# A new order of issue, a fifth buffer for turned probabilities, and the bucket table in the halves' pool, in an attention and two-MoE kernel

## The chip, the cores and the metric

One core of one Trainium2 chip runs the whole kernel in one launch. The metric is device time in microseconds (us). The kernel before was timed three times: 784.86 median (784.70, 784.86, 785.94).

## What is computed

Three stages in a chain, all in float32:

```python
# 1. attention over hash buckets: q, k, v (2, 8, 768, 64), proj (64, 6)
q_bucket = sum(((q @ proj) > 0) * 2**arange(6));  k_bucket likewise
scores = where(q_bucket == k_bucket, q @ k.T / 8, -1e9)
x = softmax(scores) @ v                      # -> (1536, 512)
# 2. first MoE layer, 512 -> 1536 -> 512
xn = x / sqrt(mean(x*x) + 1e-6) * rms_g
g = xn @ w_gate
x = (g * sigmoid(g) * (xn @ w_val)) @ w_out
# 3. second MoE layer, 512 -> 2048 -> 512
h = x @ w_in
out = where(h > 0, h, exp(min(h, 0)) - 1) @ w2_out
```

## The kernel before

Each float32 operand of a matmul is split into a rounded high part (`hi`) and the rest (`lo`), and a product takes three matmuls: hi with hi, hi with lo, lo with hi. The high part is mostly cast by ScalarE (ACT), the rest mostly subtracted by VectorE (DVE), some of both by GpSimd (POOL).

**Attention** goes over 8 pairs of heads, each with 6 units of 2 x 128 query rows. A unit is: TensorE (PE) makes the scores (`score`, L612) in PSUM; DVE takes the negative row maximum `nm` (L619); ACT the exponentials `p` (L629); PE turns `p` in three groups of four 128x128 transposes (`turn`, L657); ACT casts a turned group into a `pt` tile (L665) and DVE subtracts the rest into the same tile (L669), or for one group of some units POOL does both (L678, L681); PE multiplies by the values (`weigh`, L704). The bucket mask is made by a table of bucket counts, `wsel`: PE multiplies bits by it (`prep_count`, L539) and the result is cast into extra rows of the query and key operands (ACT L550, DVE L552). The operands' other rows come from casts and subtractions (for the first pair ACT L479 and L482, DVE L486 and L489; later queries POOL L451 and L462).

**The MoE layers** take tokens in four blocks of 384 columns and hidden features in tiles of 128. A few hidden tiles are computed plainly; the others in a Strassen-like scheme (`pair`, 9 in the first layer, 6 in the second), whose products add up in `ps_wA`, `ps_wC`, `ps_wE` (L1511). For a plain tile of the second layer, `hidden` runs: PE `ps_h` (L1060), ACT exponential and relu (L1088, L1097), DVE `hf` (L1101, "d3"), ACT cast of `h` (L1107), DVE rest of `h` (L1111). The first layer's output is reduced in `reduce1`: PE `ps_y` (L1151), DVE adds it into `ya` (L1163); with the last part added, ACT casts `y2` (L1168) and DVE subtracts the rest (L1172). The second layer's output is reduced in `reduce_cols`: PE `ps_o` (L1211), ACT copies it into `oa` (L1220) or DVE adds (L1224). `spread_t` makes differences of `ya` blocks (L1251, the first four of them on POOL) and splits them (ACT L1258, POOL L1262) for the second layer's pairs. Between the layers, plain groups 1 and 2 of the second layer (two hidden tiles each) run while the last reductions of the first layer end: the **hand-over**, some 500 to 560 us into the span. Raw weights are rounded word by word: ACT L957 ("top"), POOL L960, DVE L966, L973 and L980 (called **c3, c4, c5** here), then ACT L1005 and POOL L1009 make `whi` and `wlo`.

**The order.** `Plan.add` collects 3568 tasks with what they read and write. They are emitted in the order of a table of numbers, `ORDER` (L36):

```python
def run(self):
    assert sorted(ORDER) == list(range(len(self.tasks)))
    for i in ORDER:
        self.tasks[i][2]()
```

Each engine runs its own instructions in that order, and the tile pools add the waits for buffers. The pools that matter here:

```python
SLOTS, H3S, PTS = 22, 15, 4
...
big = ctx.enter_context(tc.tile_pool(name="big", bufs=SLOTS))
ptp = ctx.enter_context(tc.tile_pool(name="ptp", bufs=PTS))
hlf = ctx.enter_context(tc.tile_pool(name="hlf", bufs=H3S))
...
st[T_] = ptp.tile([128, 2, 512], F32R, tag="pt", name="pt")
```

`ptp` holds the `pt` tiles in attention and the `h` tiles of plain hidden tiles afterwards. `hlf` holds "halves": raw loads of queries, keys and values, POOL's `pf`, the attention output `ot`, the raw table and others. In PSUM there are two double banks (`ps_s`; for the MoE layers `ps_y` or `ps_o`) and four single banks (`ps_p`, `ps_v`, `ps_c`, `ps_h`, `ps_w...`).

Of the kernel before, what the change touches and what calls it, by code (L numbers as in the profile page):

```python
# [20 lines left out]
SLOTS, H3S, PTS = 22, 15, 4  # L21
# [254 lines left out]
def kernel(  # L276
# [41 lines left out]
    def half(shape, dtype, name):  # L318
        return hlf.tile(shape, dtype, tag="h3", name=name)
# [40 lines left out]
    def mm(n):  # L360
        return (n + 31) / 2400.0

    def dma(fn, nbytes, r=(), w=(), prio=None):
        return plan.add("SP", max(0.5, nbytes / 315e3), fn, r, w, prio, 2.3)

    st = {}

    RAW = ("qk", "kk", "qq")

# [1457 lines left out]
```

## Time and profile before

| what | value |
|---|---|
| median of 3 runs | 784.86 us |
| the profiled execution | 783.64 us, of it the span 781.9 us |
| PE busy, share of the span | 770.5 us, 99% |
| DVE, ACT, POOL busy | 663.8 (85%), 527.5 (67%), 470.8 (60%) us |
| clock granted to TensorE, mean | 1.000 |

The span runs from the first instruction to the last. Busy time is the union of an engine's instructions; matmuls are pipelined and their ends are modelled, so a row's duration can reach over the next row's start, and the starts tell more exactly when PE went on. The profiled execution is 1.22 us below the median.

### The profile page before, as it was taken

What the parts mean: (1) busy time and instruction counts of PE and PEld (TensorE: products, weight loads), DVE (VectorE), ACT (ScalarE), POOL (GpSimd) and SP (SyncE); (2) the same over time, 40 slices, a digit from 0 to 9 for tenths busy, and PEclk for the clock granted to TensorE, in tenths of its full rate; (3) what the DMA queues carried; (4) which work ended last, traced back from release to release, by engine and by line L of the source; (5) the groups of instructions that cost most, each with busy time, mean ns of one, the idle gap of its engine ahead of it and who ended that gap; (6) DMA issues with size and microseconds to landing.
All of it is one profiled execution on the core that took longest, in us unless ns stands there. A gap on an engine that the chain in (4) does not pass through costs nothing.

```text
span 781.9 us, 12995 instructions
## 1 busy us (share of the span) xinstructions
PE 770.5 (99%) x4618; PEld 726.0 (93%) x4618; DVE 663.8 (85%) x1067; ACT 527.5 (67%) x1094; POOL 470.8 (60%) x480
## 2 busy tenths in 40 slices
PE   8999999999999999999999999999999999999998
PEld 7999999989999999999999999988899889988996
DVE  7898999999995956887877887898998888898786
ACT  7999999999985536654544455567776666666652
POOL 6998889899796185554455566336364353533520
PEclk9999999999999999999999999999999999999999
DMA  4646753361010002212221122410041121131104
GB/s 169 217 141 218 255 158 106 102 183 42 6 50 1 1 1 81 82 55 74 62 80 55 55 82 81 130 60 27 1 135 54 37 72 55 54 106 56 54 1 161
DMA packets 33648, 65.73 MB, mean 84 GB/s; under 512 B 3504, under 2 KB 13104, under 8 KB 33584
## 3 DMA queue, kind: packets, MB, share of 16 engines
q1 hardware_dynamic: 33584, 64.91, 25.9%
q8 instruction: 36, 0.59, 0.3%
q14 instruction: 28, 0.23, 0.1%
HBM read 56.25 MB, written 3.15 MB: 76 GB/s over the span
## 4 chain that ended last, share of the span: by engine, by line
PE 89%; DVE 7%; ACT 2%; issue 1%; DMA 1%; SPq 0%; DVEq 0%; ACTq 0%
PE ps_o L1211 17%; PE ps_wA L1511 16%; PE ps_y L1151 12%; PE ps_h L1060 9%; PE ps_wC L1511 8%; PE ps_s L612 7%; PE ps_v L704 7%; PE ps_p L657 7%; PE ps_wE L1511 4%; DVE nm L619 1%; DVE y L1172 1%; DVE pt L669 1%; PE ps_x L762 1%; PE ps_b L520 1%; ACT p L629 1%
## 5 line engine op out<-in xcount | busy, mean ns | idle before, releaser
L1211 PE MATMUL ps_o<-whi,h 128*128 128x512 f32 (+1 forms) x388 | 119.4, 389 | 1.3 <-ACT oa L1220 1.3
L1449 POOL TENSOR_TENSOR W<-wf,W 128x256 fp32r<-128x256 f32 x105 | 85.9, 830 | 53.4 <-ACT W L1445 49.5
L1151 PE MATMUL ps_y<-h,whi 128*128 128x384 f32 x528 | 107.6, 336 | 1.1 <-DVE ya L1163 0.9
L1511 PE MATMUL ps_wA<-T,W 128*128 128x384 f32 x540 | 108.0, 335 | 0.0
L1511 PEld LDWEIGHTS ps_wA<-T,W 128*128 128x128 f32 x540 | 95.3, 188 | 2.4 <-ACT wt L1529 0.3
L1151 PEld LDWEIGHTS ps_y<-h,whi 128*128 128x128 f32 x528 | 92.5, 188 | 3.1 <-DVE ya L1163 2.5
L619 DVE TENSOR_REDUCE nm<-ps_s 128x1 f32<-128x768 f32 x96 | 90.9, 948 | 4.2 <-PE ps_s L612 3.5
L704 PE MATMUL ps_v<-pt,vv 128*128 128x256 f32 x576 | 92.8, 292 | 0.0
L629 ACT ACTIVATE p<-ps_s,nm 128x768 f32<-128x768 f32 x96 | 87.3, 910 | 2.7 <-DVE nm L619 1.6
L612 PE MATMUL ps_s<-tk,tq 128*128 128x384 f32 x384 | 87.8, 351 | 1.2 <-ACT p L629 1.2
L669 DVE TENSOR_TENSOR pt<-ps_p,pt 128x512 fp32r<-128x512 f32 x120 | 80.6, 682 | 6.1 <-ACT pt L665 4.9
L657 PE MATMUL ps_p<-ident,p 128*128 128x128 f32 x576 | 84.2, 274 | 1.0 <-DVE pt L669 0.7
L1211 PEld LDWEIGHTS ps_o<-whi,h 128*128 128x128 f32 x388 | 71.8, 188 | 13.7 <-ACT oa L1220 1.6
L704 PEld LDWEIGHTS ps_v<-pt,vv 128*128 128x128 f32 x576 | 78.2, 189 | 1.5 <-issue 0.6
L1368 POOL TENSOR_SCALAR wf<-wf 128x512 f32<-128x512 f32 x51 | 36.5, 719 | 71.5 <-ACT wf L1365 62.0
L1211 PE MATMUL ps_o<-wlo,h 128*128 128x512 f32 (+1 forms) x194 | 76.0, 392 | 0.0
L665 ACT CAST pt<-ps_p 128x512 fp32r<-128x512 f32 x120 | 69.5, 591 | 7.7 <-PE ps_p L657 4.7
L657 PEld LDWEIGHTS ps_p<-ident,p 128*128 128x128 f32 x576 | 66.9, 140 | 7.7 <-DVE pt L669 2.6
L1435 POOL TENSOR_TENSOR wf<-wf 128x256 f32<-128x256 f32 x60 | 50.1, 835 | 39.5 <-DVE wf L1384 34.3
L1224 DVE TENSOR_TENSOR oa<-ps_o,oa 128x512 f32<-128x512 f32 (+1 forms) x85 | 57.4, 679 | 17.6 <-PE ps_o L1211 17.2
L612 PEld LDWEIGHTS ps_s<-tk,tq 128*128 128x128 f32 x384 | 63.5, 189 | 4.5 <-ACT p L629 3.1
L1163 DVE TENSOR_TENSOR ya<-ps_y,ya 128x384 f32<-128x384 f32 x80 | 43.2, 551 | 15.5 <-PE ps_y L1151 15.0
(159 smaller groups left out, 1795.0 us busy)
## 6 DMA issues: line engine op xcount, KB each, us to landing
wraw<-in_moe_w_out_dram SPq DMA_DIRECT2D x25, 512.0 KB, 3.4
wraw<-in_moe_w_in_dram SPq DMA_DIRECT2D x16, 512.0 KB, 3.9
qk<-in_heads_dram SPq DMA_DIRECT2D x16, 384.0 KB, 5.2
kk<-in_heads_dram SPq DMA_DIRECT2D x14, 384.0 KB, 5.5
qq<-in_heads_dram SPq DMA_DIRECT2D x14, 384.0 KB, 5.7
wraw<-in_moe_w_gate_dram SPq DMA_DIRECT2D x18, 256.0 KB, 2.8
wraw<-in_moe_w_val_dram SPq DMA_DIRECT2D x18, 256.0 KB, 3.1
tq<-tq SPq DMA_DIRECT2D x21, 192.0 KB, 3.0
```

The lines of the kernel that those rows point to most:

```text
L612: nc.tensor.matmul(st[B_][:, hf, 0:HS], lhsT=tq[:, x, c * 128:(c + 1) * 128], rhs=tk[:, x, hf * HS:(hf + 1) * HS], start=(x == 0), stop=(x ...
L619: nc.vector.tensor_reduce(out=st["nm", u, cc], in_=st[B_][:, :, 0:HS], axis=AX.XY, op=ALU.max, negate=True,)
L629: nc.scalar.activation(out=halves(st["p", u][:, cc]), in_=st.pop(B_)[:, :, 0:HS], func=AF.Exp, bias=st["nm", u, cc], scale=1.0, accum_out= ...
L657: nc.tensor.transpose(out=st[B_][:, o:o + 128], in_=p[:, cc, (2 * n + kt) * 128:(2 * n + kt + 1) * 128], identity=ident,)
L665: nc.scalar.copy(out=st[T_][:, 0], in_=st[B_])
L669: nc.vector.tensor_tensor(out=pt[:, 1], in0=st.pop(B_), in1=f(pt[:, 0]), op=ALU.subtract)
L704: nc.tensor.matmul(st[B_][:, 0:256], lhsT=st["vv", j][:, a, 2 * n + kt, :], rhs=pt[:, x, kt * 256:(kt + 1) * 256], start=(n == seq[0] and ...
L1060: nc.tensor.matmul(ps[:, o:o + ln], lhsT=(w[wp][kk // 2][:, kk % 2] if reg2(g) else w[wp][:, kk])[:, ft * 128:(ft + 1) * 128], rhs=t[xp][: ...
L1151: nc.tensor.matmul(s["ps"][:, 0:bw], lhsT=wo[wp][:, ft if g == 0 else 0, m * 128:(m + 1) * 128], rhs=h[:, xp, 0:bw], start=(ft == 0 and i ...
L1211: nc.tensor.matmul(s["ps"], lhsT=h[:, xp, t * 128:(t + 1) * 128], rhs=(wo[wp][ft][:, 0] if reg2(g) else wo[wp][:, ft])[:, ds], start=(ft = ...
L1449: nc.gpsimd.tensor_tensor(out=t[:, 1], in0=blk(*src), in1=f(t[:, 0]), op=ALU.subtract)
L1511: nc.tensor.matmul(s[bk], lhsT=w[:, wp, k], rhs=x[:, xp, cs], start=start and k == 0 and i == 0, stop=k == 1 and i == 2, skip_group_check= ...
```

## The change

Four things change:

- `PTS` goes from 4 to 5.
- `wsel` (128 x 512 words, 2 KB a partition) is no longer a constant tile but takes one of the 15 halves, from the start until the last bucket count of the last pair of heads.
- The second plain group of the second layer takes the token blocks in the order 1, 3, 0, 2, as the first does, instead of 0, 2, 1, 3.
- `ORDER` is wholly new. It holds the same 3568 tasks, and each engine issues as many instructions of each kind as before.

```diff
-SLOTS, H3S, PTS = 22, 15, 4
+SLOTS, H3S, PTS = 22, 15, 5
...
-    wsel = const.tile([128, 2, 2, 128], F32R, name="wsel")
...
+    wsel = half([128, 2, 2, 128], F32R, "wsel")
...
-        plan.add("PE", mm(HS) + 0.02, pe, [("bits", j), "wsel"], [B_], prio)
+        plan.add("PE", mm(HS) + 0.02, pe, [("bits", j), ("h3", "wsel")], [B_], prio)
...
-    plan.add("DVE", 2.9, setup_bits, [], ["floor", "wzero"], -29)
+    plan.add("DVE", 2.9, setup_bits, [], ["floor", ("h3", "wsel")], -29)
...
-    plan.add("ACT", 0.75, spread_table, [("h3", "wtmp"), "wzero"], ["wsel"], -28)
+    plan.add("ACT", 0.75, spread_table, [("h3", "wtmp")], [("h3", "wsel")], -28)
...
-        for n, blk in enumerate((1, 3, 0, 2) if g == 1 else (0, 2, 1, 3)):
+        for n, blk in enumerate((1, 3, 0, 2) if NPW[0] % 2 else (0, 2, 1, 3)):
...
 ORDER = [
-    1, 8, 3, 0, 6, 45, 9, 7, 5, 10, 11, 12, 13, 14, 42, 43, 44, 24, 25, 2, 54, 15, 16, 71, 47, 17, 28, 29, 46, 48,
+    0, 3, 2, 1, 8, 9, 10, 11, 12, 13, 14, 15, 6, 45, 42, 44, 43, 7, 54, 5, 28, 29, 47, 49, 24, 55, 71, 16, 17, 18,
...
```

`NPW[0]` is 9 here. What the table moves at three places of the hand-over follows. A number behind a name tells tiles of one name apart; numbers of before and after are not the same.

**ScalarE, group 1 of the second layer.** `ps_o` are the first output parts of that layer, `oa` their copies, `sg`, `h` and `T` belong to hidden tiles and to the spread. Before:

```order
L1107 CAST h_6720<-hf_6680 128x384
L1088 ACTIVATE sg_6723<-ps_h_6634 128x384
L1097 ACTIVATE sg_6723<-sg_6723,ones_85 128x384
L1258 CAST T_6727<-ya_3917 128x768
L1107 CAST h_6732<-hf_6730 128x384
L1088 ACTIVATE sg_6749<-ps_h_6647 128x384
L1097 ACTIVATE sg_6749<-sg_6749,ones_85 128x384
L1088 ACTIVATE sg_6753<-ps_h_6660 128x384
L1258 CAST T_6755<-ya_3788 128x768
L1097 ACTIVATE sg_6753<-sg_6753,ones_85 128x384
L1220 COPY oa_6759<-ps_o_6683 128x512
L1220 COPY oa_6759<-ps_o_6690 128x512
```

After:

```order
L1088 ACTIVATE sg_6734<-ps_h_6656 128x384
L1107 CAST h_6736<-hf_6683 128x384
L1097 ACTIVATE sg_6734<-sg_6734,ones_84 128x384
L1107 CAST h_6742<-hf_6697 128x384
L957 ACTIVATE wf_6745<-wraw_6627 128x512
L1220 COPY oa_6749<-ps_o_6674 128x512
L1220 COPY oa_6749<-ps_o_6685 128x512
L1088 ACTIVATE sg_6753<-ps_h_6643 128x384
L957 ACTIVATE wf_6756<-wraw_6549 128x512
L1097 ACTIVATE sg_6753<-sg_6753,ones_84 128x384
L1258 CAST T_6763<-ya_3863 128x768
```

The two copies of `oa` stood behind the exponentials and relus of both hidden tiles that PE computes just before the first `ps_o`, and behind two spreads of `T`; now they stand behind those of one of these tiles and a conversion (L957), and the other tile and the `T` come after them.

**VectorE, the end of the first layer's reductions.** The last part of a weight is converted (L966, L973, L980) between adds of `ps_y`. Before:

```order
L1163 TENSOR_TENSOR ya_3917<-ps_y_6405,ya_3917 128x384
L966 TENSOR_SCALAR wf_6312<-wf_6312 128x512
L1579 TENSOR_TENSOR hf_6315<-hf_6315,wt_6380 128x384
L973 SCALAR_TENSOR_TENSOR wf_6312<-wraw_6277,wf_6312 128x512
L1163 TENSOR_TENSOR ya_3788<-ps_y_6414,ya_3788 128x384
L980 SCALAR_TENSOR_TENSOR wf_6312<-wraw_6277,wf_6312 128x512
L1163 TENSOR_TENSOR ya_3788<-ps_y_6429,ya_3788 128x384
L1579 TENSOR_TENSOR hf_6443<-ps_wA_6323,wt_6354 128x384
L1163 TENSOR_TENSOR ya_3857<-ps_y_6452,ya_3857 128x384
L1172 TENSOR_TENSOR y2_6424<-ya_3917,y2_6424 128x384
```

After:

```order
L966 TENSOR_SCALAR wf_6374<-wf_6374 128x512
L1579 TENSOR_TENSOR hf_6359<-hf_6359,wt_6381 128x384
L973 SCALAR_TENSOR_TENSOR wf_6374<-wraw_6331,wf_6374 128x512
L1163 TENSOR_TENSOR ya_3863<-ps_y_6391,ya_3863 128x384
L1532 TENSOR_TENSOR wt_6344<-ps_wE_6413,wt_6344 128x384
L1163 TENSOR_TENSOR ya_3759<-ps_y_6422,ya_3759 128x384
L980 SCALAR_TENSOR_TENSOR wf_6374<-wraw_6331,wf_6374 128x512
L1172 TENSOR_TENSOR y2_6430<-ya_3759,y2_6430 128x384
L1579 TENSOR_TENSOR hf_6446<-ps_wA_6297,wt_6344 128x384
L1163 TENSOR_TENSOR ya_3759<-ps_y_6451,ya_3759 128x384
```

Before, `ya_3917` is the add that the first subtraction of `y2` (L1172) waits for, and all three conversions stand behind it; now `ya_3759` is that add, L966 and L973 stand ahead of it, and only L980 stands behind it.

**VectorE, the hidden tiles of block 3.** `hf` (L1101) is what ScalarE casts into `h` and VectorE subtracts from. Before:

```order
L1101 SCALAR_TENSOR_TENSOR hf_6680<-ps_h_6612,sg_6625 128x384
L1111 TENSOR_TENSOR h_6584<-hf_6582,h_6584 128x384
L1172 TENSOR_TENSOR y2_6542<-ya_3857,y2_6542 128x384
L966 TENSOR_SCALAR wf_6677<-wf_6677 128x512
L1111 TENSOR_TENSOR h_6720<-hf_6680,h_6720 128x384
L973 SCALAR_TENSOR_TENSOR wf_6677<-wraw_6609,wf_6677 128x512
L1101 SCALAR_TENSOR_TENSOR hf_6730<-ps_h_6634,sg_6723 128x384
L1111 TENSOR_TENSOR h_6732<-hf_6730,h_6732 128x384
```

After:

```order
L1101 SCALAR_TENSOR_TENSOR hf_6683<-ps_h_6603,sg_6616 128x384
L1172 TENSOR_TENSOR y2_6521<-ya_3876,y2_6521 128x384
L1101 SCALAR_TENSOR_TENSOR hf_6697<-ps_h_6629,sg_6693 128x384
L966 TENSOR_SCALAR wf_6596<-wf_6596 128x512
L1172 TENSOR_TENSOR y2_6503<-ya_3759,y2_6503 128x384
L973 SCALAR_TENSOR_TENSOR wf_6596<-wraw_6594,wf_6596 128x512
L966 TENSOR_SCALAR wf_6731<-wf_6731 128x512
L1111 TENSOR_TENSOR h_6742<-hf_6697,h_6742 128x384
L973 SCALAR_TENSOR_TENSOR wf_6731<-wraw_6729,wf_6731 128x512
L1111 TENSOR_TENSOR h_6736<-hf_6683,h_6736 128x384
```

The second `hf` of the block stood behind L966, a subtraction of `h` and L973; now it stands ahead of them.

## Rows read from the trace of the kernel before

**Rows 1.** The page, part 1: busy us, share of span, instructions.

```profile
PE 770.5 (99%) x4618; PEld 726.0 (93%) x4618; DVE 663.8 (85%) x1067; ACT 527.5 (67%) x1094; POOL 470.8 (60%) x480
```

**Rows 2.** Busy time by stretch: PE, PEld, DVE, ACT, POOL, clock, DMA.

```profile
160.00:180.00 20.00, 19.03 (x145) 17.07 (x144) 19.82 (x31) 18.23 (x37) 18.28 (x16) 1.00 0.51 160
...
200.00:220.00 20.00, 19.25 (x141) 18.24 (x140) 19.65 (x29) 19.39 (x43) 16.22 (x17) 1.00 0.09 27
...
500.00:520.00 20.00, 19.01 (x102) 17.03 (x101) 19.55 (x38) 9.51 (x21) 4.56 (x5) 1.00 0.33 106
...
540.00:560.00 20.00, 18.03 (x92) 16.03 (x91) 16.08 (x22) 15.19 (x30) 8.32 (x5) 1.00 0.09 27
```

**Rows 3.** Timeline of PE, hand-over: start, us, line, operation, [idle before <- releaser].

```profile
510.18 0.85 PE L1511 MATMUL ps_wA<-T,W 128*128 128x384 f32 x4
510.87 1.21 PE L1151 MATMUL ps_y<-h,whi 128*128 128x384 f32 x6
512.26 2.38 PE L1151 MATMUL ps_y<-h,whi 128*128 128x384 f32 x12 [0.18 <-DVE ya L1163]
515.17 1.31 PE L1151 MATMUL ps_y<-h,whi 128*128 128x384 f32 x6 [0.53 <-DVE ya L1163]
516.66 2.22 PE L1151 MATMUL ps_y<-h,whi 128*128 128x384 f32 x9 [0.18 <-DVE ya L1163]
...
541.33 0.34 PE L1060 MATMUL ps_h<-y,wlo 128*128 128x384 f32 x1
542.97 0.73 PE L1211 MATMUL ps_o<-whi,h 128*128 128x512 f32 x2 [1.31 <-ACT oa L1220]
...
552.56 0.34 PE L1060 MATMUL ps_h<-y,wlo 128*128 128x384 f32 x1
553.56 0.61 PE L1060 MATMUL ps_h<-y,whi 128*128 128x384 f32 x2 [0.66 <-DVE hf L1101]
```

**Rows 4.** Timeline of ACT, hand-over.

```profile
539.28 0.51 ACT L1107 CAST h<-hf 128x384 fp32r<-128x384 f32 x1 [3.43 <-DVE hf L1101]
...
542.35 1.06 ACT L1220 COPY oa<-ps_o 128x512 f32<-128x512 f32 x2
...
546.71 0.52 ACT L1107 CAST h<-hf 128x384 fp32r<-128x384 f32 x1
```

**Rows 5.** Timeline of DVE, hand-over.

```profile
508.55 0.41 DVE L966 TENSOR_SCALAR wf<-wf 128x512 int32<-128x512 int32 x1
...
509.36 0.68 DVE L973 SCALAR_TENSOR_TENSOR wf<-wraw,wf 128x512 int32<-128x512 int32 x1
509.96 0.54 DVE L1163 TENSOR_TENSOR ya<-ps_y,ya 128x384 f32<-128x384 f32 x1
510.43 1.31 DVE L980 SCALAR_TENSOR_TENSOR wf<-wraw,wf 128x512 int32<-128x512 int32 x1
...
525.12 2.68 DVE L1172 TENSOR_TENSOR y<-ya,y 128x384 fp32r<-128x384 f32 x2
...
534.80 2.08 DVE L966 TENSOR_SCALAR wf<-wf 128x512 int32<-128x512 int32 x1
```

**Rows 6.** Timeline of POOL, hand-over.

```profile
525.35 2.04 POOL L1251 TENSOR_TENSOR ya<-ya 128x768 f32<-128x768 f32 x1 [0.42 <-DVE ya L1163]
```

**Rows 7.** Timeline of PE, one place in attention.

```profile
161.64 0.60 PE L657 MATMUL ps_p<-ident,p 128*128 128x128 f32 x4
162.45 0.66 PE L657 MATMUL ps_p<-ident,p 128*128 128x128 f32 x4 [0.21 <-DVE ot L722]
162.86 0.94 PE L612 MATMUL ps_s<-tk,tq 128*128 128x384 f32 x4
164.27 0.66 PE L657 MATMUL ps_p<-ident,p 128*128 128x128 f32 x4 [0.47 <-DVE pt L669]
```

**Rows 8.** Timeline of DVE at the start.

```profile
9.22 0.60 DVE L489 TENSOR_SCALAR tq<-qk 64x768 fp32r<-64x768 f32 x1
```

**Rows 9.** Loads of raw queries (tile qq), us from issue to landing.

```profile
DMA to landing us min/median/max: 3.1/5.7/7.5
```

372 rows, old and new, of the table ORDER are left out of this document.

## Prediction

> **What bounds the kernel now.** I read the busy shares first. PE works 770.5 us of a span of 781.9, 99% [rows 1]. No instruction is added or removed, so PE's work stays, and at most the 11.4 us that PE is idle, and what lies hidden in stretched rows, can go. DVE comes next with 85%: it is no bound over the whole, but may be one in a stretch. So I read busy time by stretches of 20 us [rows 2]. Two kinds of stretch are short of PE work. In attention PE has 19.03 in 160 to 180 and 19.25 in 200 to 220, where DVE has 19.82 and 19.65: there DVE is full and PE waits for it. In the hand-over PE has 19.01 in 500 to 520, where DVE is full again (19.55), and 18.03 in 540 to 560, where no engine is full (DVE 16.08, ACT 15.19): there single instructions stand at the wrong place in a queue. Third, I read the timelines of PE, ACT, DVE and POOL in the hand-over, since the change shows there most plainly.
>
> PE's pace comes from two starts: four matmuls of 384 columns start at 510.18 and the next row at 510.87, so 0.69 / 4 = 0.173 us each [rows 3]. What a start is late by that pace is a loss, also where "idle" shows less. Three losses result:
> - **ps_o**: one matmul from 541.33 on, the next at 542.97: 1.64 - 0.17 = 1.47 lost. PE waited for ACT's copy of `oa` to free a double bank. That copy ran at 542.35, behind the exponentials and a `T`, which stood behind a cast of `h` at 539.28 that had waited 3.43 for `hf` [rows 4]. `hf` was late since DVE stood in L966 for 2.08 from 534.80 [rows 5].
> - **ps_h**: 552.56 to 553.56, 1.00 - 0.17 = 0.83 lost, waiting for `hf` [rows 3]. Further back stands ACT's cast of block 0's `h`, which came only at 546.71 [rows 4], and DVE's queue had the subtraction that needs this cast ahead of the `hf`. The cast needs an `h` tile, and all four tiles of the pool held `h` of blocks 1 and 3 until PE's last `ps_o` on one of them: this is where a fifth tile counts.
> - **ps_y**: the rows with 6, 12 and 6 matmuls from 510.87 should take 1.04, 2.08 and 1.04, and take 1.39, 2.91 and 1.49 [rows 3]: 0.35 + 0.83 + 0.45 = 1.63 lost, waiting for DVE's adds.
>
> **The change, part by part.**
> *Copies of oa moved forward on ACT.* In the new order they stand behind one exponential and relu less and ahead of the `T`. ACT's cast before them needs the `hf` that DVE now issues ahead of L966, not behind it. Both links of the chain of the 1.47 us are cut, and the exponential that is delayed belongs to a tile whose `ps_o` comes many matmuls later. I take the whole 1.47; bounds 0 (another instruction of the same queue is late instead) and -1.47.
>
> *Fifth tile.* The cast of block 0's `h` need no longer wait for PE's last use of blocks 1 and 3. I take the 0.83; bounds 0 and -0.83. In attention, the fifth tile lets ACT's casts run further ahead of the weighing. There PE's waits name DVE (an `ot` add, a `pt` subtraction) [rows 7], not a tile, so I take nothing from it there.
>
> *Weight conversions at the end of layer one.* L966 takes 0.41 at 508.55, L973 holds DVE from 509.36 to the next start at 509.96, 0.60, and L980 takes 1.31 at 510.43, all behind the add that the first `y2` needs [rows 5]. Now the first two, 1.0, stand ahead of it; of the third I count 0.68, as long as its like L973's row, 0.6 less. DVE being full [rows 2], work taken out of this stretch shortens PE's waits one for one until they are gone: 1.0 + 0.6 = 1.6 of the 1.63. I take -1.5, since a row's duration reaches a little over the next start; bounds 0 (the work before that add is late instead) and -1.63.
>
> *The start.* On DVE both halves of an operand's L489 now come before L552, whose result the first scores need; before, one stood behind. That is one instruction of 0.60 [rows 8] ahead of the first score. By the fourth row maximum DVE has done the same work in both orders, so part of it is regained. I take +0.3; bounds 0 and +0.6.
>
> *Block order of group 2.* The same matmuls on the same weights in another order, in a stretch where PE loses nothing after 560 us: 0. Its cover is that group 1 has freed its banks; without it, it would be the 1.47 of one late `ps_o` copy.
>
> *wsel in a half.* No engine works for it. It takes one of 15 halves until the last count. Following the tasks' order, 7 to 13 halves are live through most of attention, so it binds nothing; only the raw load of one query (pair 5) has to wait for a half. Raw queries land in 3.1 to 7.5 us, median 5.7 [rows 9]. At the median it comes in time for POOL, at the longest 1.8 later: bounds 0 and +1.8. I take 0.
>
> *The rest of attention.* The new order swaps neighbours all over it. In the place of rows 7, four transposes start at 161.64 and the next ones at 162.45, 0.81 where the next four take 0.41 (162.45 to 162.86); four scores from 162.86 should end at 163.55 and the next row starts at 164.27. So 0.40 + 0.72 = 1.12 is lost in one such place, to DVE. The new order has the same DVE work there and moves some ACT casts ahead of an exponential. I see no place that is clearly better and take 0, with bounds of two such places, -2.2 and +2.2.
>
> The **sum** is -1.47 - 0.83 - 1.5 + 0.3 = -3.5. The profiled execution took 783.64 (span 781.9 and 1.74 around it), so 780.1 by it; it lies 1.22 below the median of 784.86, so the median would be 781.4, 0.4% less. About 0.2%, 1.57 us, is what a measurement of this kernel can tell from no change.
>
> **The rivals.**
> *The gain is given back in the hand-over.* DVE's subtraction of two `y2` tiles at 525.12 took 2.68, where about 1.1 would do (two of the 0.54 of an add of the same size at 509.96): it ran beside a difference on POOL from 525.35, 2.04 long [rows 5, 6]. L966 at 534.80 took 2.08 against 0.41 at 508.55 [rows 5]. So a DVE instruction that meets one of POOL's four long differences is held by 1.6 to 1.7. The Trainium skill, page "SBUF — State Buffer", section "Who interferes with whom", has for this an exclusive lock on a shared port pair: a DVE instruction with two SBUF inputs and a GpSimd instruction that reads SBUF exclude each other, and the later one waits for all of the other. By that rule the holds don't shrink with a better order, they only fall on other instructions, which the two rows bear out. The new order keeps all four differences on POOL and has more SBUF-only DVE work (L966, L973, subtractions) in a row behind the second `hf`. If two more holds, 3.3, fall on `y2` or `hf` that PE waits for, the sum is -0.2: 784.7. Against it: I reckon some 4 us between the last `y2` and its use in the new order, so it takes three holds on one path before PE feels one.
>
> *Slower: DVE falls behind in attention.* With five tiles, transposes and casts may run ahead, and L669's subtractions come before row maxima, for which the exponentials and with them the next transposes wait. Where DVE has 19.65 to 19.82 of 20 [rows 2], it can't make up what it does too early. If each of the seven stretches from 80 to 220 lost one place of 1.12 as 160 to 180 does, that is six more, 6.7, and with the gains above -3.5 + 6.7 = +3.2: 788.1. It decides from about five places up (5 x 1.12 - 3.5 = +2.1). Against it: the order is fixed, so the tiles alone can't bring a subtraction ahead of a maximum; only the table can, and where I compared the two orders, the distances from a score to its turning are much the same.
>
> *Attention gains too.* If the losses of 160 to 180 and 200 to 220, 0.97 and 0.75 short of 20 [rows 2], go as well, -1.7: 779.7. The new order weighs later after turning in most units, which speaks for it; the full DVE speaks against.
>
> *The change doesn't do what it says.* The fifth tile may never be in use when ACT wants it, since the order holds ACT's cast back anyway. Then the 0.83 stays: 782.2. This still is faster.
>
> **How the numbers follow.** The forecast, together with the one that only lacks the fifth tile's share: 0.55. Attention gains too: 0.07. Given back: 0.23. Slower: 0.15. So faster 0.62, same 0.23, slower 0.15. The likeliest time is 781.4. Its own range, by the bounds of the terms, is about 779 to 784. The range for 8 in 10 goes down to 778.5 (attention's bound, -2.2, beyond the forecast is 779.2, and a little for the spread of runs) and up to 786.5, which takes in the given-back case and leaves out most of the slower one.
>
> **What would show it.** Right: PE's wait for ACT's `oa` and that for `hf` in the hand-over are gone, those for `ya` shrink to a few tenths by starts, and PE's busy time in the three stretches from 500 to 560 (shifted by what came before) is near 20. ACT's cast of `h` no longer waits 3.43 for `hf`. Wrong: new waits of PE for `y2` or `hf` beside long DVE rows that start within a POOL difference (given back); or PE under 19.5 in several stretches from 80 to 220 with waits for `p`, `pt` or `nm` (slower); or PE waiting for a raw query in pair 5 (the table's half).

## The result: 1.3% slower

The changed kernel takes 795.07 us (median of 4 runs, 794.49 to 796.34) where the kernel before takes 784.78 beside it: ratio 1.0132, 95% interval 1.0114 to 1.0149. Forecast were 781.4, and 778.5 to 786.5 as the range; the change is slower by 10.3 us.

### The profile after

The page, part 1, of the changed kernel, span 792.6 us, against [rows 1]:

```profile
PE 772.2 (97%) x4618; PEld 727.5 (92%) x4618; DVE 673.1 (85%) x1067; ACT 522.8 (66%) x1094; POOL 466.9 (59%) x480
```

The counts are the same. PE is busy 1.7 us more and the span is 10.7 us longer. DVE is busy 9.3 us more for the same 1067 instructions: some of them got longer. The groups by line show which. First the changed kernel:

```profile
L966 DVE TENSOR_SCALAR wf<-wf 128x768 int32<-128x768 int32 x6 | 11.0, 1831 | 0.0
```

then the kernel before:

```profile
L966 DVE TENSOR_SCALAR wf<-wf 128x768 int32<-128x768 int32 x6 | 5.3, 884 | 0.0
```

Six instructions in attention account for 5.7 of the 9.3 us. Busy time by stretch says where PE lost (columns as in [rows 2]), in the changed kernel:

```profile
100.00:120.00 20.00, 16.22 (x114) 15.39 (x116) 18.91 (x23) 14.25 (x30) 12.60 (x11) 0.91 0.39 119
...
160.00:180.00 20.00, 18.59 (x133) 16.95 (x131) 19.84 (x29) 17.47 (x37) 15.70 (x13) 1.00 0.51 159
180.00:200.00 20.00, 18.61 (x140) 17.03 (x141) 19.40 (x30) 16.21 (x33) 18.22 (x16) 1.00 0.21 52
...
520.00:540.00 20.00, 18.02 (x97) 16.20 (x96) 19.87 (x33) 11.95 (x23) 7.29 (x6) 1.00 0.16 57
540.00:560.00 20.00, 20.00 (x106) 18.51 (x105) 19.50 (x23) 14.86 (x30) 13.51 (x10) 1.00 0.08 26
```

and the first of them in the kernel before:

```profile
100.00:120.00 20.00, 19.88 (x151) 18.62 (x150) 19.61 (x30) 19.28 (x41) 17.77 (x17) 1.00 0.53 159
```

PE's worst stretch is 100 to 120, with 16.22, and the granted clock has 0.91 there, the only stretch under 1.00. By the starts of its matmuls against their pace, as the prediction did it, PE loses 11.4 us more than before from 20 to 340 us (10 to 12 more, by how the pace of each kind of matmul is taken); past 340 it lost 7.8 and loses 7.6. So the loss is in attention and the first MoE pairs, and all that follows, the hand-over included, on which the prediction rested, gave 0.2. Here is the worst place on PE, DVE and POOL:

```profile
102.62 1.04 PE L657 MATMUL ps_p<-ident,p 128*128 128x128 f32 x8
107.44 0.69 PE L539 MATMUL ps_c<-bitt,wsel 128*128 128x384 f32 x1 [3.78 <-DVE pt L669]
...
101.85 4.93 DVE L966 TENSOR_SCALAR wf<-wf 128x768 int32<-128x768 int32 x1
106.70 0.68 DVE L669 TENSOR_TENSOR pt<-ps_p,pt 128x512 fp32r<-128x512 f32 x1
...
101.34 1.83 POOL L462 TENSOR_TENSOR tq<-qq,tq 64x768 fp32r<-64x768 f32 x1
103.12 0.60 POOL L678 CAST pt<-pf 128x512 fp32r<-128x512 f32 x1
103.69 1.46 POOL L789 TENSOR_TENSOR sq<-xT 128x768 f32<-128x768 f32 x1
105.11 1.25 POOL L681 TENSOR_TENSOR pt<-pf,pt 128x512 fp32r<-128x512 f32 x1
```

One L966, 0.55 us of work, takes 4.93: it starts while POOL is in L462 and ends 0.4 us after POOL's fourth instruction in a row (106.36). Such a DVE instruction, which takes longer than its work beside one of POOL, is called held from here on, and what it takes too long a hold. Behind it in DVE's queue stands the subtraction L669, which frees the bank that PE's next matmul needs; PE stands for 3.78. Before, the same L966 came two DVE instructions later, at 103.34, in a pause of POOL from 102.69 to 103.88, and took 0.55:

```profile
103.34 0.55 DVE L966 TENSOR_SCALAR wf<-wf 128x768 int32<-128x768 int32 x1
...
101.77 0.92 POOL L451 TENSOR_SCALAR tq<-qq,share 128x768 fp32r<-128x768 f32 x1
103.88 0.61 POOL L678 CAST pt<-pf 128x512 fp32r<-128x512 f32 x1 [1.20 <-ACT pt L665]
```

And PE comes back at half clock in the changed kernel; busy time by stretch again, with the clock as the first number behind the engines:

```profile
103.00:107.40 4.40, 0.66 (x7) 0.42 (x4) 4.40 (x3) 1.52 (x4) 3.36 (x4) 1.00 0.20 45
107.40:108.00 0.60, 0.56 (x2) 0.56 (x3) 0.60 (x1) 0.00 (x0) 0.00 (x0) 0.50 0.00 0
...
109.00:110.00 1.00, 1.00 (x4) 1.00 (x4) 0.92 (x2) 0.99 (x3) 0.56 (x2) 0.50 0.15 37
110.00:111.00 1.00, 1.00 (x7) 1.00 (x7) 0.70 (x1) 0.00 (x0) 1.00 (x1) 0.60 1.11 197
111.00:112.00 1.00, 1.00 (x9) 1.00 (x8) 0.69 (x2) 0.86 (x3) 1.00 (x2) 1.00 0.83 283
```

After this idle time the granted clock is 0.50 (1.2 GHz) until between 110 and 111, then 1.00 again: 3.4 us at half clock cost about 1.7 us. The place costs some 5.6 us in all. Six more conversions in attention took 1.4 to 2.5 us beside POOL, each followed by a loss of PE of 0.7 to 1.7.

Not all of the 11.4 us is in attention. In the first MoE pairs a subtraction, L1111, with some 0.55 us of work, is held beside POOL; the `hf` behind it comes late, ACT's cast and copy behind that too, and PE waits once:

```profile
311.83 2.19 DVE L1111 TENSOR_TENSOR h<-hf,h 128x384 fp32r<-128x384 f32 x1
...
308.90 4.72 POOL L1320 TENSOR_TENSOR T<-xT,T 128x768 fp32r<-128x768 f32 x2 [1.49 <-ACT T L1316]
...
316.21 0.62 PE L1151 MATMUL ps_y<-h,whi 128*128 128x384 f32 x2 [1.02 <-ACT ya L1159]
```

Before, PE has no wait from 255 to 345 us.

### The profile page after: what moved, and what is told of

It reads as the page before. It is cut to its first block, busy times and chain, and to the rows that moved or that the text cites. A ratio compares the mean times of both kernels' runs of the same rounds, so it can differ in the third digit from the quotient of the medians.

```text
span 792.6 us, 13004 instructions
## 1 busy us (share of the span) xinstructions
PE 772.2 (97%) x4618; PEld 727.5 (92%) x4618; DVE 673.1 (85%) x1067; ACT 522.8 (66%) x1094; POOL 466.9 (59%) x480
## 4 chain that ended last, share of the span: by engine, by line
PE 72%; DVE 17%; ACT 6%; issue 3%; DMA 1%; POOL 0%; ACTq 0%; DVEq 0%; POOLq 0%
PE ps_o L1211 16%; PE ps_wA L1511 15%; PE ps_y L1151 10%; PE ps_wC L1511 8%; PE ps_h L1060 6%; PE ps_s L612 4%; PE ps_p L657 4%; PE ps_v L704 4%; PE ps_wE L1511 4%; DVE pt L669 3%; DVE nm L619 3%; ACT p L629 2%; ACT pt L665 2%; DVE wf L966 1%; DVE y L1172 1%
## 5 line engine op out<-in xcount | busy, mean ns | idle before, releaser
L704 PE MATMUL ps_v<-pt,vv 128*128 128x256 f32 x576 | 94.4, 293 | 0.2 <-DVE pt L669 0.2
L669 DVE TENSOR_TENSOR pt<-ps_p,pt 128x512 fp32r<-128x512 f32 x120 | 80.2, 682 | 10.3 <-ACT pt L665 9.7
L657 PE MATMUL ps_p<-ident,p 128*128 128x128 f32 x576 | 81.3, 274 | 4.6 <-DVE pt L669 3.2
L704 PEld LDWEIGHTS ps_v<-pt,vv 128*128 128x128 f32 x576 | 80.2, 191 | 2.1 <-DVE pt L669 1.1
L1435 POOL TENSOR_TENSOR wf<-wf 128x256 f32<-128x256 f32 x60 | 47.8, 797 | 49.6 <-DVE wf L1384 48.6
```

What stands on the lines that cost most here:

```text
L657: nc.tensor.transpose(out=st[B_][:, o:o + 128], in_=p[:, cc, (2 * n + kt) * 128:(2 * n + kt + 1) * 128], identity=ident,)
L669: nc.vector.tensor_tensor(out=pt[:, 1], in0=st.pop(B_), in1=f(pt[:, 0]), op=ALU.subtract)
L704: nc.tensor.matmul(st[B_][:, 0:256], lhsT=st["vv", j][:, a, 2 * n + kt, :], rhs=pt[:, x, kt * 256:(kt + 1) * 256], start=(n == seq[0] and ...
```

## Experiments

Theory 1: the order of attention puts VectorE's conversions beside long GpSimd work, which holds them, and PE pays. Rivals: the pools cost; the hand-over costs; VectorE simply falls behind there. Each ratio is to the kernel before, timed beside it. In the order diffs each row is an instruction, in its engine's order.

| run | us | ratio, 95% interval |
|---|---|---|
| h1_early_old | 785.69 | 1.0018 (1.0009 to 1.0028) |
| h2_early_new | 794.95 | 1.0139 (1.0123 to 1.0154) |
| p5_pools_only | 785.45 | 1.0014 (1.0004 to 1.0024) |
| e13_half_only | 786.02 | 1.0024 (1.0015 to 1.0034) |
| c3_one_port | 795.36 | 1.0142 (1.0127 to 1.0157) |
| e5_one_c3_moved | 789.80 | 1.0064 (1.0051 to 1.0078) |
| e6_shorter_run | 790.78 | 1.0079 (1.0060 to 1.0097) |
| e16_run_reordered | 791.45 | 1.0092 (1.0076 to 1.0109) |
| e7_eight_moved | 787.84 | 1.0041 (1.0028 to 1.0055) |
| e9_hold_put_in | 785.83 | 1.0012 (1.0003 to 1.0021) |
| e14_gapless_run | 785.97 | 1.0027 (1.0016 to 1.0038) |
| e8_before_copies_first | 783.08 | 0.9983 (0.9974 to 0.9992) |
| e10_fifth_tile_used | 785.00 | 0.9998 (0.9989 to 1.0007) |
| e11_before_three_more | 782.84 | 0.9973 (0.9962 to 0.9983) |
| e15_hf_first | 781.71 | 0.9970 (0.9959 to 0.9981) |
| e12_later_difference | 785.93 | 1.0012 (1.0002 to 1.0021) |

### Which part of the change

```diff
 h1: ORDER = before[:1761] + [i for i in after if i not in before[:1761]]
 h2: ORDER = after[:1761] + [i for i in before if i not in after[:1761]]
```

> The changed kernel with the first 1761 places of the table (attention and the first MoE pairs) in the order of before, and all other tasks in the new order; five tiles, table in a half, new block order. Theory 1 (the loss sits in the new order of attention, where VectorE's weight conversions meet long GpSimd runs): 784.5 us, since the start-to-start losses of PE up to 340 us were 14.8 before and 25.7 after, and past it 7.8 and 7.6. Rival (the pools, or the hand-over, make it slower): about 795 us.

> The reverse: the first 1761 places in the new order, the rest in the order of before with its block order; five tiles, table in a half. Theory 1: about 795 us, all of the loss. Rival (hand-over): 785 us.

785.69 and 794.95: the first 1761 places carry the loss, about as large with the old hand-over as with the new. h1 lies 1.2 us above what was expected, no more than the half alone costs in the old order (e13 below).

```diff
 p5: ORDER of before
-SLOTS, H3S, PTS = 22, 15, 4
+SLOTS, H3S, PTS = 22, 15, 5
...
-    wsel = const.tile([128, 2, 2, 128], F32R, name="wsel")
...
+    wsel = half([128, 2, 2, 128], F32R, "wsel")
...
 e13: the same without the first pair of lines
```

> The kernel before, order and block order untouched, with five tiles and the table in a half. Theory 1 (the order alone is slower): 784 to 785 us; if the fifth tile frees ScalarE's cast of h in the hand-over, PE's wait for hf there (0.83 us) goes and it is 784.0. Rival (the fifth tile or the half costs): 787 us or more, with new waits in attention.

> The kernel before with the table in a half, four tiles, old order: the half alone. Theory (the half costs: ScalarE's L957 at about 80 waits for GpSimd to free a half, PE then waits 0.8 us for p): the same new wait as with both pool changes, 0.1% over before, about 785.4 us. Rival (the fifth tile costs): no such wait, as before.

In the old order the pools cost 0.1 to 0.2%, not 1.3%: nearly nothing, but the half is not free. Timeline of ACT and PE in p5 (its lines stand 8 lower than those quoted so far):

```profile
81.79 0.94 ACT L949 ACTIVATE wf<-wraw 128x768 f32<-128x768 f32 x1 [1.46 <-POOL tq L454]
...
83.66 0.55 PE L649 MATMUL ps_p<-ident,p 128*128 128x128 f32 x3 [0.83 <-ACT p L621]
```

ACT's conversion waits until POOL frees a half; exponentials stand behind it, and PE waits for one. The run with the half alone has the same wait, so it is the half and not the tile: 0.1 to 0.2%. In the new order this wait is not there. The new order was not tried with four tiles, nor with the table outside the halves.

### Is it the hold, and what sets its length

```diff
 e5, VectorE of the changed kernel:
 L980  (of the weight before, 95.0)
+L966
...
 L722
-L966  (101.85)
 L669
```

> The changed kernel with one VectorE instruction moved: the L966 that took 4.93 us at 101.85 stands some 7 us earlier, right behind the L980 of the weight before, where GpSimd waits for VectorE. Theory 1 (the length is a hold by GpSimd, not the work): it takes 0.55 us, and PE's gap of 3.94 us with the half-clock stretch behind it (about 1.7 us) go: 789 to 790 us; the other holds stay. Rival (VectorE's queue there is too full whatever the place of L966): 793 us or more.

```profile
96.51 0.55 DVE L966 TENSOR_SCALAR wf<-wf 128x768 int32<-128x768 int32 x1
```

0.55 us, as expected, and 789.80 us: this one instruction's place is 5.3 of the 10.3 us. Shown.

```diff
 c3_one_port, the changed kernel:
+                wo = wi
+                if g == 0:
+                    wo = wi.rearrange("p a b -> p (a b)")
+                    if shape[1] != 3:
+                        wo = wo.rearrange("p (a b) -> p a b", a=3)
...
-                    out=wi, in0=wi, scalar1=0x07FFFFFF, scalar2=3,
+                    out=wo, in0=wi, scalar1=0x07FFFFFF, scalar2=3,
```

> The changed kernel; only the six wide L966 conversions get views of unlike outer dimensions for input and output (3 x 256 against 768, or 2 x 384 against 3 x 256), the same elements in the same order. Theory 1 with the port rule (a two-port mode makes L966 wait for GpSimd): L966 takes about 0.9 us, never more than 1.1, the 4.93 us one is gone and with it PE's gap of 3.9 us and the half-clock stretch behind it (1.7 us): 787 to 790 us. Rival 1 (a conversion there delays VectorE whatever its mode): over 793 us. Rival 2 (GpSimd's run holds L966 in any mode): L966 still takes 4.9 us, 795 us.

Nothing changed (4.92 us at the place), and neither did the L966 that no one holds (0.54 at 172.4 in this run): with these views of the same bytes the instruction is as long as before. The edit did not bring about what it was to test, so the run does not tell the theories apart.

```diff
 e6, GpSimd of the changed kernel:
 L462
 L678
-L789
 L681
 L740
+L789
 e16, GpSimd of the changed kernel:
 L462
+L789
 L678
-L789
 L681
```

> The changed kernel with one GpSimd instruction moved and L966 left at its place: the L789 inside the run of four GpSimd instructions beside it (1.46 us) stands behind the run and the next wait. Theory 1a (the hold lasts until GpSimd's run ends): L966 takes about 3.5 us instead of 4.93, PE's gap shrinks by 1.4. Theory 1b (the hold is that by one GpSimd instruction and something else adds to it): still 4.9 us.

> The changed kernel with two GpSimd instructions exchanged beside the L966 that took 4.93 us: L789 now ahead of the cast L678; the same four instructions, L966 at its place. Theory 1 (which instruction follows decides: after L462 an L678 lets VectorE not in, an L789 does, as in e14): L966 takes 1.9 to 2.3 us, PE's gap falls from 3.9 to about 1 us, no half clock: 790 to 791 us. Rival (the run as a whole holds it): about 4.9 us again, 795 us.

L966 in e6, then in e16, then PE's wait in e16:

```profile
102.05 2.27 DVE L966 TENSOR_SCALAR wf<-wf 128x768 int32<-128x768 int32 x1
```

```profile
101.72 3.16 DVE L966 TENSOR_SCALAR wf<-wf 128x768 int32<-128x768 int32 x1
...
105.53 0.45 PE L539 MATMUL ps_c<-bitt,wsel 128*128 128x384 f32 x1 [2.01 <-DVE pt L669]
```

and the clock of e16 behind that wait:

```profile
105.50:107.00 1.50, 1.47 (x10) 1.47 (x11) 1.50 (x3) 0.62 (x1) 1.20 (x1) 1.00 0.00 0
```

With VectorE's order untouched, GpSimd's order alone sets the length: 4.93, 3.16, 2.27 us, and the time follows it, 795.1, 791.5, 790.8 us (e5, 0.55 us: 789.8). In e16 the clock stayed at 1.00 behind an idle time of 2.01; so from 4.93 to 3.16 more is won (3.6 us) than the hold got shorter (1.8), and from 4.93 to 2.27 too (4.3 and 2.7): the difference is the 1.7 of the clock. This is the traced execution; another one of e16, of 793.45 us, has a mean clock of 0.998 like that of the changed kernel, where the other three have 1.000, so an idle time like this one may not keep the clock every time; where it fell there is not recorded. Both expectations were off in the length: in e6 L966 got in after L678, at a gap of 0.09 us before L681, and not at the end of the run; in e16 after L789, where there is no gap, and L678 was the one to wait (0.94 us for 0.60).

```diff
 e9, the kernel before:
 VectorE: L722
+L966
 L669
 L619
-L966  (103.34)
 GpSimd: L451
+L462
 L678
-L462
+L789  (stood ahead of L451 by three)
 L681
-L793
 L1009, L740
+L793
 e14: as e9, with L789 between L462 and L678
```

> The kernel before, its pools and order, with the one meeting of the changed kernel put into it: on VectorE the L966 of about 103.3 stands two instructions earlier (ahead of the subtraction L669 and the maximum L619 it followed), and on GpSimd L462 and L678 stand ahead of L789 and L681 so that they run without a gap. Theory 1 (that meeting alone makes most of the loss): L966 takes 3 to 5 us, PE waits 2.5 to 4 us for L669 at about 103, and the clock may fall: 787 to 790 us. Rival (it needs the rest of the new order too): 784 to 785.5 us.

> As e9, but on GpSimd L789 stands between L462 and L678, so that two instructions without a dependence follow each other without a gap beside the L966 of about 102. Theory 1a (L966 waits until GpSimd's run has a gap): L966 takes 3.3 us or more and PE waits over 1.5 us for L669. Theory 1b (it waits for one instruction): 1.9 us as in e9.

Both cost 1 to 2 us (785.83 and 785.97), not 4 to 5: the transplant to this one place does not make the loss again. In both L966 is held by one instruction alone. In e9 GpSimd paused 0.74 for ScalarE behind L462. In e14 it went on without a gap, yet:

```profile
102.10 1.92 DVE L966 TENSOR_SCALAR wf<-wf 128x768 int32<-128x768 int32 x1
...
101.77 1.83 POOL L462 TENSOR_TENSOR tq<-qq,tq 64x768 fp32r<-64x768 f32 x1
103.57 1.78 POOL L789 TENSOR_TENSOR sq<-xT 128x768 f32<-128x768 f32 x1
```

Here L966 got in at the end of L462 and L789 was held (1.78 for 1.46). So a run without a gap holds it sometimes by one instruction, sometimes by more, even where the same L789 follows the same L462 (e14 and e16); what decides was not found.

### The rest of attention

```diff
 e7, VectorE of the changed kernel, besides the L966 of e5:
-L966 of 73.4, 140.4, 223.1; L973 of 117.6; L980 of 123.0, 169.4, 180.4
+L966 behind the L619 of 75.5, behind the L619 of 144.9, ahead of the L973 of 221.6
+L973 behind the second L669 of 113.8
+L980 behind the L669 of 115.4, behind the L669 of 171.6, behind the L973 of 175.0
```

> The changed kernel with eight weight conversions of attention (three L966, one L973, three L980 and the one of the run before) moved on VectorE by one to a few places, to where GpSimd waits in its trace. PE's losses next to the long ones sum to 12.7 us (0.75, 5.6, 0.7, 1.3, 1.6, 1.4, 1.3). Theory 1: most of it goes, 783 to 787 us. Rival (the new order lets VectorE fall behind by its turns and maxima, conversions only show it): 788 us or more, with new waits for pt and nm.

787.84: 7.2 us of the loss are back, less than expected. A new hold came up:

```profile
108.38 2.04 DVE L973 SCALAR_TENSOR_TENSOR wf<-wraw,wf 128x768 int32<-128x768 int32 x1
```

and PE waited 1.21 for a DVE subtraction in this stretch: the place of that L973 was chosen in a trace that shifted with the other moves. In 160 to 176 PE waits for L669 and the exponential by 2.0 us in all without a hold beside them (before, it was idle for 0.97 in 160 to 180 [rows 2]), which leaves a part of the loss to the order itself. The hold of L1111 in the first MoE pairs, with PE's wait of 1.02, is unchanged in this run: no run moved it by itself.

### The prediction's terms, one by one

```diff
 e8, the kernel before: VectorE
-L966
 L1111
-L973
 L1101  hf of block 3, second
+L966
+L973
 ScalarE
+L1220 oa, L1220 oa
 L1088, L1088, L1258, L1097 of block 0
-L1220 oa, L1220 oa
```

> The kernel before, four tiles, with what the prediction named for the hand-over and nothing else: on VectorE the second hf of block 3 ahead of L966 and L973; on ScalarE the first two copies of oa ahead of the exponentials of block 0. By the prediction's term PE's wait of 1.47 us for the copy of oa goes: about 783.0 us against 784.3. Rival (given back at the next wait, the 0.83 us one for hf grows): 784.3 us.

783.08: the first term is right, alone and in its size (1.3 us). PE's remaining wait for `hf` in that run was 0.9. POOL's difference now holds L1111 where it held L966 (2.21 us at 536.84), ahead of the `hf` as before; ACT's cast waited 1.67 for it, not 3.43.

```diff
 e10 = p5 + e8, ScalarE
+L1107 h of block 0
 L1220 oa
 L1220 oa
-L1107
 e15 = e11, VectorE
-L1251
+L1101 hf of block 2
 L1111
+L1101 hf of block 2
+L1251
 L973
-L1101, L1101
```

> The kernel before with five tiles and the table in a half (785.45 us in its own run), with the moves of e8 and one more: ScalarE's cast of block 0's h ahead of the two copies of oa that it stood behind, which four tiles would not allow. By the prediction's second term, put right (the tile alone does nothing, the tile with the cast moved does): PE's wait of 0.83 us for hf goes beside the 1.47 for oa, 785.45 - 1.3 - 0.85 = about 783.3 us. Rival (hf is late for another reason): about 784.1 us and the wait stays.

> The kernel before with the moves of e8 and three conversions of attention moved later on VectorE, to where GpSimd waits in the trace of before: L966 of 134.1, L980 of 162.3, L966 of 203.5. Theory 1: their holds of 0.8, 0.4 and 0.9 go, PE's losses next to them (0.4 to 1.0 each at 162 and 206) shrink: 782 to 782.8 us against 783.1. Rival (VectorE is full there, a hold less in one place is one more in another): 783.1 us or more.

> e11 with the two hf (L1101) of block 2 moved ahead of a difference (L1251) and an L973 on VectorE, four tiles. Theory (the 0.83 us wait is VectorE's order, the fifth tile isn't needed): PE's wait for hf in the hand-over falls from 1.0 to under 0.3 us, about 782.1 us where e11 has 782.84 and before 784.8. Rival: the wait stays or another takes its place, 782.8 us.

In p5, with five tiles and the old order, PE's waits for `oa` (1.3) and `hf` (0.7) stood as before. In e10 the one for `hf` is gone and the one for `oa` is down to 0.3, but the time is 785.00, not the 783.3 expected: by the ratios 0.16% less than p5, what e8 gave alone, so the term for `hf` does not show in the time; this order still pays for the half. In e15 the wait for `hf` is gone with four tiles, by VectorE's order alone: 781.71 us, 0.30% faster than before and the best of all, though not clear of e11 (0.27%) by the intervals. e11 moves three conversions out of holds, by the same method as e7 but in the trace of before (L966 of 134.1, L980 of 162.3, L966 of 203.5 to places where GpSimd pauses); with e8 it gives 0.27% where e8 gives 0.17%, which the intervals do not keep apart. e15's own waits of PE:

```profile
PE ps_w L1659 <- POOL ident masks.py:199: 1.3, 1, 1.3
PE ps_s L612 <- ACT p L629: 0.9, 3, 0.4
PE ps_y L1151 <- DVE ya L1163: 0.9, 3, 0.5
...
```

Neither `oa` nor `hf` is left in this list.

```diff
 e12 = h1, GpSimd
-L1251  (second difference)
 L1262
+L1251
```

> The run with the early order of before and the new late order (785.7 us), with two GpSimd instructions of the hand-over exchanged: the second long difference (L1251) behind the L1262 that followed it. Theory: VectorE's L1172 of 527.0 then takes 0.55 us, not 2.00, and PE's wait of 0.9 us for that y2 goes: about 784.7 us. Rival (another hold falls on the same path): 785.5 us or more.

The changed kernel's hand-over shows what this was for:

```profile
535.64 2.01 DVE L1172 TENSOR_TENSOR y<-ya,y 128x384 fp32r<-128x384 f32 x1
...
535.40 1.84 POOL L1251 TENSOR_TENSOR ya<-ya 128x768 f32<-128x768 f32 x1 [1.03 <-PE ps_h L1060]
...
537.70 0.44 PE L1060 MATMUL ps_h<-y,whi 128*128 128x384 f32 x1 [0.89 <-DVE y L1172]
```

In e12 that hold and that wait are gone, and the exchanged difference held the next L1172:

```profile
526.13 0.54 DVE L1172 TENSOR_TENSOR y<-ya,y 128x384 fp32r<-128x384 f32 x1
...
530.73 2.27 DVE L1172 TENSOR_TENSOR y<-ya,y 128x384 fp32r<-128x384 f32 x1 [0.32 <-ACT y L1168]
...
530.74 1.84 POOL L1251 TENSOR_TENSOR ya<-ya 128x768 f32<-128x768 f32 x1
...
551.97 0.61 PE L1060 MATMUL ps_h<-y,whi 128*128 128x384 f32 x2 [1.46 <-DVE hf L1101]
```

785.93 us, no better than h1: the rival's case. PE's wait for `hf` at 551.97 is new (in h1 none for it is over 0.4); by the starts, PE's loss in 540 to 560 grew from 0.7 to 1.8, as much as was won before it.

## Why the prediction was wrong

- **Attention at 0, bounds 2.2 either way.** This is the step that failed. By starts 11.4 us were lost from 20 to 340, some 10 of them in attention and 1.2 in the first MoE pairs, for the most part by holds of DVE beside POOL and, in one place, the clock behind a hold. The prediction compared distances from scores to turnings, and what DVE has to do; it did not look at what POOL does while DVE does it, though it had priced such a hold at 1.6 to 1.7 us from [rows 5, 6] for the hand-over. Attention has 18 wide conversions, DVE at 18.5 to 19.8 of 20 and POOL at 16 to 19 from 80 to 240 before: every place of a conversion in the new order needed the same look, in the orders of both engines.
- **The price of a hold.** A row of 2.08 gave 1.7 as what a hold costs. The worst one cost 4.4 on DVE, and 5.6 on PE with the clock: over twice attention's bound in one place. The slow ends of all terms add up to +4.6, 789.5 us, not to the 784 that the prediction gives for them, and the 795.07 measured lies beyond that too.
- **The slower rival** (0.15, 788.1 us) had the place right, attention with a full DVE, and PE's waits for `pt`; its mechanism, subtractions ahead of maxima by the fifth tile, is not what e5, e6 and e16 show, and it named at most 1.12 us for one place. Whether it has a share of what e7 leaves is not shown.
- **Copies of oa, -1.47: right.** The wait is gone in the changed kernel, and e8 shows 1.3 us alone.
- **Fifth tile, -0.83: wrong cause.** The tile alone does nothing (p5). The wait goes with the tile and a moved cast (e10), or with DVE's order and no tile (e15), and in neither does its 0.8 us show in the time clear of noise. In the changed kernel 0.6 us for `hf` remained.
- **Conversions at the end of layer one, -1.5: given back.** PE's waits for `ya` are 1.2 us where they were 0.9: L966 and L973 did move, but L980, at 520.87, took 1.65 beside a POOL instruction, not the 0.68 counted.
- **Given back in the hand-over** (0.23, 784.7): this rival's size came out for all past attention. Of its mechanism, two L1172 are held by POOL's differences, but only one has a wait of PE behind it (0.89); it had counted on two. Its sentence that holds don't shrink with a better order, and only fall on other instructions, fits e8 and e12, where another instruction was held; it does not fit e5, where L966 in a pause of POOL took 0.55 and 5.3 us were won. The late order alone is worth 0.2% slower in h1 with the half, and e13 has 0.24% for the half by itself: nothing net.
- **wsel in a half, 0, bounds 0 and +1.8.** In the old order it binds, 0.14 to 0.24%, but on a weight conversion of ACT and not on the query load named.
- **The start, +0.3.** Not seen: PE's first score started at 9.01 to 9.73 us in the traces with the new early order, and at 9.26 to 10.14 in those with the old.

## What to carry to other kernels

When a table moves instructions on VectorE and GpSimd, lay the two queues beside each other: a VectorE instruction with SBUF operands alone (none in PSUM) may cost its own length plus that of what GpSimd runs beside it, and on a full VectorE PE pays it. Put such work where GpSimd waits (e5), and take the places from a trace a few at a time, since each move shifts the next meeting (e7, e12). An idle time of PE is priced together with the clock that it gets behind it.

## What was not expected of the hardware

- L966 was passed over by up to three GpSimd instructions after the first. The Trainium skill, page "SBUF — State Buffer", section "Who interferes with whom", lets the one that comes second wait until the first finishes. Most holds here end so: 2.08 beside the difference of 2.15 before, 1.92 in e14. The 4.93, 3.16 and 2.27 us do not: there a later GpSimd instruction went first again. The measurement decides, and what chooses between the two is open. The prediction spoke of instructions with two SBUF inputs; L966 has one and is held all the same.
- PE idle for 3.78 us came back with a granted clock of 0.50 for 3.4 us; PE idle for 2.01 us at the same place came back at 1.00 in the traced execution of e16.
